# Attention with an off-by-one softmax and a cosine router on one core: one transposition for the rests of q and k, a shorter router product, and GpSimd's adds tied to VectorE

## The chip, the cores and the metric

The kernel runs on one core of a Trainium2 chip, as one launch. The metric is the device time in microseconds (us) of that launch; lower is better. A profile is one execution recorded by the hardware profiler. In it PE is TensorE (PEld its weight loads), DVE is VectorE, ACT is ScalarE, POOL is GpSimd, and SP is SyncE, which here only issues transfers. A Q behind an engine's name (POOLq) is that engine's instruction queue.

## What is computed

First attention over 8 batches, 12 heads, 448 positions and head size 64, whose softmax has an extra term in its denominator. Its result, laid out as 3584 tokens of 768 numbers, goes through a router that picks one of 8 experts for each token by cosine similarity, and through that expert's two layers.

```python
def _attn_ref(q, k, v):                      # (8, 12, 448, 64) each
    scores = scale * np.matmul(q, k.transpose(0, 1, 3, 2))
    m = np.max(scores, axis=-1, keepdims=True)
    e = np.exp(scores - m)
    attn = e / (np.sum(e, axis=-1, keepdims=True) + np.exp(-m) + 1e-09)
    return np.matmul(attn, v)

def _moe_ref(x, expert_emb, tau, w1, w2):    # N, D, E, F = 3584, 768, 8, 1024
    xn = x / (np.linalg.norm(x, axis=-1, keepdims=True) + 1e-06)
    en = expert_emb / (np.linalg.norm(expert_emb, axis=-1, keepdims=True) + 1e-06)
    logits = xn @ en.T / tau
    expert_idx = np.argmax(logits, axis=1)
    # ... gate_w: the softmax probability of the chosen expert ...
    for e in range(E):
        h = np.maximum(x[mask] @ w1[e], 0.0)
        out[mask] = gate_w[mask, None] * (h @ w2[e])
```

## The kernel before

The kernel is one hand-made schedule. Work is cut into 48 head pairs g (six to a batch); a pair has eight slots of program order. `put(slot, fn)` files a piece of work under a place in that order, and the pieces are emitted by ascending slot. So slots fix the order in which each engine gets its instructions; they are not times. Every engine runs its own queue in order.

448 positions are three blocks of 128 and a rest of 64. Scores are made transposed: keys on partitions, queries along the row, and the two heads of a pair on the two halves of the array's rows. For a pair: q and k are transposed on TensorE into PSUM, `kt` is copied out by ScalarE and `qt` by VectorE; three score blocks j (both heads each) and one block for the rests of both heads go through the exponential on ScalarE and a subtraction of one on VectorE (`em`, `emx`); `attend` multiplies them with v; `recip` makes the reciprocal denominator in two ScalarE steps (`rd`); `normalise` makes x on VectorE.

```python
LAG = 2 * NP                                   # NP = 6 pairs a batch
FILL = ((2.8, 5.3, 5.4), (2.8, 5.4))
...
    nc.gpsimd.tensor_tensor(out=vs[:], in0=vs[:], in1=t.v[:, :, 2, :], op=ALU.add)
    nc.gpsimd.tensor_tensor(out=vs[:], in0=vs[:], in1=t.v[:, :, 3, :], op=ALU.add)
    k.va[n] = vs


def front_qk(k, g, s):
    nc = k.nc
    n, i = g // GP, g % GP
    t = k.ld[n]
    ps = k.big.tile([128, 2, 512], F32, name="big", tag="big")
    for m, x, r in ((0, t.qm, t.qr[:, 2 * i : 2 * i + 2, :]), (1, t.km, t.kr[:, i, :])):
        for j in range(3):
            nc.tensor.transpose(ps[:, m, 128 * j : 128 * j + 128], x[:, j, 2 * i : 2 * i + 2, :], k.ident[:])
        nc.tensor.transpose(ps[:, m, SM:512], r, k.ident[:])
    def k_out():
        kt = k.qt.tile([128, 512], F32R, name="kt", tag="kt")
        nc.scalar.copy(out=kt[:], in_=ps[:, 1, :])
        k.kts[g] = kt

    def q_out():
        qt = k.qt.tile([128, S], F32R, name="qt", tag="qt")
        nc.vector.tensor_copy(out=qt[:], in_=ps[:, 0, 0:S])
        k.qts[g] = qt
    k.put(s + 1.1, k_out)
```

The rest of k was loaded into a tile of zeros with the two heads on the diagonal (rows 0 to 63 in columns 0 to 63, rows 64 to 127 in columns 64 to 127), so its transposition puts zeros beside each head. The rest of q has its own tile, of which half the rows are zero.

```python

    k.put(pa, exp)


def attend(k, g, s):

    nc = k.nc
    va = k.vab[g % 2]
    ps = k.av.tile([128, 2, 512], F32, name="av", tag="av")
    for h in range(2):
        r = slice(64 * h, 64 * h + 64)
        nc.tensor.matmul(
            ps[:, h, 0:S], lhsT=va[r, 3, h : h + 2, :], rhs=k.ems[g, 3][r, :], start=True, stop=False,
        )
    for j in range(3):
        for h in range(2):
            nc.tensor.matmul(
                ps[:, h, 0:S], lhsT=va[:, j, h : h + 2, :], rhs=k.ems[g, j][:, h, :],
                start=False, stop=(j == 2),
            )

    i = g % GP
    nc.tensor.matmul(ps[:, 0, S : S + 1], lhsT=k.va[g // GP][:, 2 * i : 2 * i + 2, :], rhs=k.ones_f[:], start=True, stop=True)
    rd = k.rdp.tile([128, 2, S], F32, name="rd", tag="rd")
    k.avs[g] = ps, rd

    def recip():
        nc.scalar.activation(rd[:], ps[:, :, 0:S], ACT.Ln, bias=1.0, scale=1.0 / (S + 1.0))
        nc.scalar.activation(rd[:], rd[:], ACT.Exp, scale=-1.0)

    k.put(s + 2.3, recip)
```

The router needs, for each token, the products with the 8 expert embeddings and the sum of squares over all six x of a batch. Four products run side by side on 32 columns of the array each, q = 0 and 1 with the embeddings, q = 2 and 3 with ones and the squares:

```python


def square(k, g):
    x = k.xs[g]
    xs = k.xsp.tile([128, S], F32, name="xs", tag="xs")
    if g < LAG - 1:
        k.nc.gpsimd.tensor_tensor(out=xs[:], in0=x[:], in1=x[:], op=ALU.mult)
    else:
        k.nc.scalar.activation(xs[:], x[:], ACT.Square)
    k.xs[g] = (x, xs)


def router_mm(k, b, s):

    nc = k.nc
    ps = k.big.tile([128, 512], F32, name="rmm", tag="big")
    for r in range(3):
        for q in range(4):
            c = 3 * (q % 2) + r
            x = k.xs[b * NP + c][q // 2]
            nc.tensor.matmul(
                ps[32 * q : 32 * q + 32, 0:S], lhsT=(k.en[:, c, :] if q < 2 else k.ones32[:]), rhs=x[:],
                start=(r == 0), stop=(r == 2),
            )
    for c in range(NP):
        k.xs.pop(b * NP + c)
    k.put(s + 1.9, lambda: nc.scalar.copy(out=k.rr[:, 0:S], in_=ps[:, 0:S]))

```

The result is copied by ScalarE, transposed in four pieces (`router_tok`), and VectorE finds the best expert of each token. Tokens are counted by a matmul with ones, the expert with most tokens in the batch is read into a GpSimd register, and GpSimd then fetches that expert's weights in seven transfers. Its layers, the MoE of the batch, are 15 chunks of matmuls (8 of the first layer, 7 of the second), which fill TensorE between the steps of attention pairs from LAG pairs on. Until then, dummy matmuls on the identity (`warm`) stand in their place. Where tokens choose other experts, a loop at the end adds those; the counts decide that while the kernel runs.

```python
# in pipeline(k)
    for n in range(NG * B):                    # a load covers two pairs
        ...
        put(s + 1.2, lambda n=n: sum_v(k, n))  # three GpSimd adds over v
    for g in range(G):
        s = g * NSLOT
        put(s - NSLOT + 4.2, lambda g=g, s=s - NSLOT + 4.2: front_qk(k, g, s))
        put(s + 0.8, lambda g=g: front_v(k, g))
        for j, o, pa, pv in ((0, 0, 0.3, 1.5), (1, 0.05, 0.4, 2.6), (2, 5.2, 6, 7.7), (3, 0.15, 2.6, 7)):
            put(s + o, lambda g=g, j=j, pa=s + pa, pv=s + pv: scores(k, g, j, pa, pv))
        s += NSLOT
        put(s + 0.1, lambda g=g, s=s: attend(k, g, s + 0.1))
        put(s + 4.75, lambda g=g, s=s: normalise(k, g, s + 4.75))
        put(s + 7.1, lambda g=g: square(k, g))
    put(-NSLOT, lambda: warm(k, 24))
    ...
# PSUM pools: work 2 x 1 bank, big 2 x 2 banks, av 1 x 2 banks
```

The softmax here doesn't subtract the row's maximum and nothing guards it: scores larger than these inputs give would overflow.

## Time and profile before

| what | value |
|---|---|
| time, median of 3 | 430.42 us (430.19 to 431.25) |
| span of the profiled execution | 430.1 us |
| instructions | 7384 |
| mean transfer rate | 162 GB/s |

A line of a group gives the kernel's line, the engine and operation, the tile written and the tiles read, their shape and type and how often it ran; behind the bar the busy time in us and the mean of one in ns, and then the idle time of the engine just before them and who ended most of it. The mean of a matmul is its latency, not its distance from the next. A line of the chain in order of time gives start, length and what ran; the chain is followed back from the last instruction, at each step to what released it. VectorE's largest groups, for instance:

```profile
L241 DVE TENSOR_SCALAR em<-e 128x896 fp32r<-128x896 f32 x144 | 96.9, 687 | 7.2 <-ACT e L233 6.8
L286 DVE SCALAR_TENSOR_TENSOR x<-av,rd 64x448 f32<-64x448 f32 x96 | 66.3, 691 | 46.7 <-ACT rd L274 36.4
L200 DVE CAST qt<-big 128x448 fp32r<-128x448 f32 x48 | 29.9, 624 | 24.1 <-ACT kt L195 22.8
```

Here x waited 46.7 us in all, mostly for the reciprocal rd, and qt 24.1 us, mostly for the end of ScalarE's copy kt.

### The profile page before, as it was taken

Reading aid. Unit: us, or ns where it says so; the run is one execution under the profiler, and the core shown is the slowest. Engines: PE = TensorE matmul, PEld = TensorE weight load, DVE = VectorE, ACT = ScalarE, POOL = GpSimd, SP = SyncE. Lnnn points to the kernel's source line nnn. Section 1 sums busy time; section 2 is a strip of 40 time slices with the busy share of each in tenths; the row PEclk is TensorE's granted clock in tenths of the full one; section 3 lists DMA queues with packets and bytes.
Section 4 is the critical chain, followed back from the end, with each engine's and each line's share of the span. In section 5 each row is a group of like instructions: output and inputs, shape, how many; then the busy total and the mean of one; then the engine's idle time right before and its main releaser. Section 6 shows DMA issues by size and latency. Waiting matters only on the chain.

```text
span 430.1 us, 7384 instructions
## 1 busy us (share of the span) xinstructions
PE 400.0 (93%) x2430; PEld 248.1 (58%) x2430; DVE 314.8 (73%) x658; ACT 305.3 (71%) x440; POOL 171.7 (40%) x242
## 2 busy tenths in 40 slices
PE   8878987879999999999999999999999999998885
PEld 3555554646556656665666656665666566644443
DVE  1697878789689769887787868976988778754222
ACT  1777776777788977978788878897698878751111
POOL 4043315754359106740377024910675037504500
PEclk9998999899999999999999999999999999999999
DMA  8775552997489964998399938997499508853973
GB/s 168 175 179 123 131 128 65 179 181 158 99 173 216 257 164 96 232 198 232 81 232 199 254 96 152 218 240 198 79 230 203 170 2 135 160 131 52 231 141 130
DMA packets 133690, 69.76 MB, mean 162 GB/s; under 512 B 99849, under 2 KB 127497, under 8 KB 133649
## 3 DMA queue, kind: packets, MB, share of 16 engines
q1 hardware_dynamic: 115392, 43.63, 40.0%
q0 software_dynamic: 16384, 25.17, 34.6%
q10 hardware_dynamic: 1872, 0.46, 0.6%
q8 instruction: 20, 0.33, 0.3%
q14 instruction: 22, 0.17, 0.1%
HBM read 83.39 MB, written 16.52 MB: 232 GB/s over the span
## 4 chain that ended last, share of the span: by engine, by line
PE 56%; DVE 20%; ACT 11%; issue 5%; POOL 4%; DMA 3%; POOLq 1%; DVEq 0%; ACTq 0%
PE av L262 11%; PE work L513 10%; PE work L485 8%; PE big L222 7%; DVE x L286 5%; PE big L191 4%; PE rmm L317 4%; DVE em L241 4%; DVE qt L200 4%; ACT e L233 3%; ACT rd L274 3%; DMA w<-in_moe_w_dram 3%; ACT rd L273 3%; PE work L629 2%; PE work L532 2%
## 5 line engine op out<-in xcount | busy, mean ns | idle before, releaser
L233 ACT ACTIVATE e<-big 128x896 f32<-128x896 f32 x144 | 127.6, 921 | 32.1 <-PE big L222 31.4
L241 DVE TENSOR_SCALAR em<-e 128x896 fp32r<-128x896 f32 x144 | 96.9, 687 | 7.2 <-ACT e L233 6.8
L286 DVE SCALAR_TENSOR_TENSOR x<-av,rd 64x448 f32<-64x448 f32 x96 | 66.3, 691 | 46.7 <-ACT rd L274 36.4
L485 PE MATMUL work<-xb,w 128*128 128x448 bf16 x384 | 79.7, 353 | 1.3 <-DMA w<-in_moe_w_dram 0.8
L262 PE MATMUL av<-em,vab 128*128 128x448 f32 x288 | 73.1, 391 | 0.0
L513 PE MATMUL work<-w,h 128*128 128x384 bf16 x384 | 68.4, 326 | 4.8 <-DMA w<-in_moe_w_dram 2.0
L222 PE MATMUL big<-qt,kt 64*128 64x448 f32 x288 | 56.8, 435 | 15.8 <-DVE qt L200 15.0
L357 POOL TENSOR_TENSOR nrm<-nrm,half 128x4 f32<-128x4 f32 x8 | 8.5, 1068 | 134.0 <-DVE nrm L339 134.0
L262 PEld LDWEIGHTS av<-em,vab 128*128 128x128 f32 x288 | 51.5, 192 | 16.2 <-issue 13.1
L485 PEld LDWEIGHTS <-w 128*128 128x128 bf16 x384 | 34.9, 98 | 39.4 <-issue 9.8
L273 ACT ACTIVATE rd<-av 128x896 f32<-128x896 f32 x48 | 44.1, 919 | 17.4 <-PE av L268 11.2
L445 POOL DMA_DIRECT2D w<-in_moe_w_dram x56 | 45.2, 809 | 27.0 <-issue 23.0
L513 PEld LDWEIGHTS <-h 128*128 128x128 bf16 x384 | 35.5, 98 | 31.5 <-issue 9.3
L222 PEld LDWEIGHTS big<-qt,kt 64*128 64x128 f32 x288 | 24.3, 184 | 43.1 <-ACT e L233 14.4
L200 DVE CAST qt<-big 128x448 fp32r<-128x448 f32 x48 | 29.9, 624 | 24.1 <-ACT kt L195 22.8
L274 ACT ACTIVATE rd<-rd 128x896 f32<-128x896 f32 x48 | 45.7, 952 | 1.5
L195 ACT CAST kt<-big 128x512 fp32r<-128x512 f32 x48 | 28.1, 585 | 12.1 <-PE big L192 12.0
L503 DVE TENSOR_SCALAR y<-work,g 128x384 f32<-128x384 f32 x32 | 19.6, 614 | 15.4 <-PE work L513 11.2
L629 PE MATMUL work<-ident 128*128 128x512 bf16 x96 | 28.6, 426 | 2.0 <-POOL ident masks.py:199 1.7
L493 DVE TENSOR_SCALAR h<-work 128x448 bf16<-128x448 f32 x40 | 24.6, 617 | 6.8 <-PE work L485 6.7
L209 DVE CAST vab<-vld 128x512 fp32r<-128x512 f32 x48 | 29.4, 612 | 0.0
L303 POOL TENSOR_TENSOR xs<-x 128x448 f32<-128x448 f32 x11 | 10.3, 933 | 40.5 <-DVE x L286 34.7
(103 smaller groups left out, 569.2 us busy)
## 6 DMA issues: line engine op xcount, KB each, us to landing
w<-in_moe_w_dram POOLq DMA_DIRECT2D x24, 512.0 KB, 7.9
w<-in_moe_w_dram POOLq DMA_DIRECT2D x32, 384.0 KB, 7.8
qm<-in_q_dram SPq DMA_DIRECT2D x72, 128.0 KB
vld<-in_v_dram SPq DMA_DIRECT2D x24, 384.0 KB
out_dram<-y SPq DMA_DIRECT2D x48, 192.0 KB
km<-in_k_dram SPq DMA_DIRECT2D x69, 128.0 KB
qrest<-in_q_dram SPq DMA_DIRECT2D x24, 64.0 KB
vld<-in_v_dram SPq DMA_DIRECT2D x48, 32.0 KB
```

What stands on the lines that cost most here:

```text
L200: nc.vector.tensor_copy(out=qt[:], in_=ps[:, 0, 0:S])
L222: nc.tensor.matmul(ps[:, h, 0:S], lhsT=kt[64 * h : 64 * h + 64, 128 * j : 128 * j + 128], rhs=qt[64 * h : 64 * h + 64, :], start=True, sto ...
L233: nc.scalar.activation(e[:], ps[:, :, 0:S], ACT.Exp, scale=scale)
L241: nc.vector.tensor_scalar_sub(em[:], e[:], 1.0)
L262: nc.tensor.matmul(ps[:, h, 0:S], lhsT=va[:, j, h : h + 2, :], rhs=k.ems[g, j][:, h, :], start=False, stop=(j == 2),)
L273: nc.scalar.activation(rd[:], ps[:, :, 0:S], ACT.Ln, bias=1.0, scale=1.0 / (S + 1.0))
L274: nc.scalar.activation(rd[:], rd[:], ACT.Exp, scale=-1.0)
L286: nc.vector.scalar_tensor_tensor(out=x[r, :], in0=ps[r, h, 0:S], scalar=ps[r, 0, S : S + 1], in1=rd[o, h, :], op0=ALU.add, op1=ALU.mult,)
L445: k.nc.gpsimd.dma_start(w[:], src)
L485: nc.tensor.matmul(ps[:, 0:S], lhsT=w1[c // 2][:, c % 2, 128 * f : 128 * f + 128], rhs=xb[:, c, :], start=(c == 0), stop=(c == NP - 1),)
L513: nc.tensor.matmul(ps[:, 0:SM], lhsT=hs[f][:, 128 * t : 128 * t + 128], rhs=w2[f // 2][:, f % 2, SM * n : SM * n + SM], start=(f == 0), st ...
L629: nc.tensor.matmul(ps[:], lhsT=idb[:, 0:128], rhs=idb.unsqueeze(1).broadcast_to([128, 2, 256]), start=True, stop=True)
```

## The change

Five things are done together. The rests of q and k of a head are loaded one above the other (q on rows 0 to 63, k on rows 64 to 127) and go through one transposition; two small VectorE copies put k's part into `kt`, which now has two fixed buffers whose zeros are written once. The squares of pairs 1 to 4 of a batch are added up on VectorE onto the first one, so that the router product has two accumulation steps instead of three. GpSimd's adds and squares get a dependence on the last subtraction of one on VectorE, so that they run while VectorE reads PSUM. The product for the rest scores of the next pair stands between the two parts of `attend`. And the slots of several pieces move: `qt` now stands ahead of `normalise`, MoE starts one pair earlier (LAG 11) with another spread of its chunks, and the router's later steps come later. The diff, cut where only names or the same lines move:

```diff
 NG = 3
-LAG = 2 * NP
-FILL = ((2.8, 5.3, 5.4), (2.8, 5.4))
+LAG = 2 * NP - 1
+FILL = 2 * ((2.8, 5.3, 5.4),) + ((2.8,), (2.8, 5.4)) + 2 * ((2.8, 5.3, 5.4),)
 NSLOT = 8
...
 def build_consts(k):
...
-        kr = pool.tile([128, GP, 128], F32, name=f"krest{s}")
-        nc.vector.memset(kr[:], 0.0)
...
+        kt = pool.tile([128, 512], F32R, name=f"kt{s}")
+        for h in range(2):
+            nc.vector.tensor_scalar_mul(
+                kt[64 * h : 64 * h + 64, S - 64 * h : 512 - 64 * h], k.ones_f[64 * h : 64 * h + 64, 0:1].broadcast_to([64, 64]), 0.0
+            )
+        k.kt.append(kt)
...
             )
-    nc.sync.dma_start(t.qr[0:64, :, :], k.q[b, h0 : h0 + 2 * GP, SM:S, :].rearrange("h p d -> p h d"))
-    keng.dma_start(t.kr[0:64, :, 0:64], rest2(k.k, 0))
-    keng.dma_start(t.kr[64:128, :, 64:128], rest2(k.k, 1))
+    for eng, h, src in ((nc.sync, 0, k.q), (keng, 1, k.k)):
+        eng.dma_start(t.r[64 * h : 64 * h + 64, :, :], src[b, h0 : h0 + 2 * GP, SM:S, :].rearrange("h p d -> p h d"))
     k.ld[n] = t
...
-def sum_v(k, n):
+def sum_v(k, n, js):
     nc, t = k.nc, k.ld[n]
-    vs = k.vsp.tile([128, 2 * GP, DH], F32, name="vs", tag="vs")
-    nc.gpsimd.tensor_tensor(out=vs[:], in0=t.v[:, :, 0, :], in1=t.v[:, :, 1, :], op=ALU.add)
-    nc.gpsimd.tensor_tensor(out=vs[:], in0=vs[:], in1=t.v[:, :, 2, :], op=ALU.add)
-    nc.gpsimd.tensor_tensor(out=vs[:], in0=vs[:], in1=t.v[:, :, 3, :], op=ALU.add)
-    k.va[n] = vs
+    if js[0] == 1:
+        k.va[n] = k.vsp.tile([128, 2 * GP, DH], F32, name="vs", tag="vs")
+    vs = k.va[n]
+    for j in js:
+        k.behind(nc.gpsimd.tensor_tensor(out=vs[:], in0=(vs[:] if j > 1 else t.v[:, :, 0, :]), in1=t.v[:, :, j, :], op=ALU.add))
...
     t = k.ld[n]
-    ps = k.big.tile([128, 2, 512], F32, name="big", tag="big")
-    for m, x, r in ((0, t.qm, t.qr[:, 2 * i : 2 * i + 2, :]), (1, t.km, t.kr[:, i, :])):
+    pq = k.big.tile([128, 512], F32, name="tq", tag="big")
+    pk = k.work.tile([128, 512], F32, name="tk", tag="work")
+    for ps, x in ((pq, t.qm), (pk, t.km)):
         for j in range(3):
-            nc.tensor.transpose(ps[:, m, 128 * j : 128 * j + 128], x[:, j, 2 * i : 2 * i + 2, :], k.ident[:])
-        nc.tensor.transpose(ps[:, m, SM:512], r, k.ident[:])
+            nc.tensor.transpose(ps[:, 128 * j : 128 * j + 128], x[:, j, 2 * i : 2 * i + 2, :], k.ident[:])
+        if x is t.qm:
+            nc.tensor.transpose(pq[:, SM:512], t.r[:, 2 * i : 2 * i + 2, :], k.ident[:])
+    kt = k.kt[g % 2]
+    k.kts[g] = kt
+
     def k_out():
-        kt = k.qt.tile([128, 512], F32R, name="kt", tag="kt")
-        nc.scalar.copy(out=kt[:], in_=ps[:, 1, :])
-        k.kts[g] = kt
+        nc.scalar.copy(out=kt[:, 0:SM], in_=pk[:, 0:SM])
...
         qt = k.qt.tile([128, S], F32R, name="qt", tag="qt")
-        nc.vector.tensor_copy(out=qt[:], in_=ps[:, 0, 0:S])
+        nc.vector.tensor_copy(out=qt[:], in_=pq[:, 0:S])
         k.qts[g] = qt
+
+    def r_out():
+        for h in range(2):
+            r = slice(64 * h, 64 * h + 64)
+            nc.vector.tensor_copy(out=kt[r, SM + 64 * h : S + 64 * h], in_=pq[r, S:512])
+
     k.put(s + 1.1, k_out)
-    k.put(s + 2.1, q_out)
+    k.put(s + 0.5, q_out)
+    k.put(s + 0.5, r_out)
...
-            nc.vector.tensor_scalar_sub(em[:], e[:], 1.0)
+            k.last = nc.vector.tensor_scalar_sub(em[:], e[:], 1.0)        # emx likewise
...
         )
-    for j in range(3):
-        for h in range(2):
-            nc.tensor.matmul(
-                ps[:, h, 0:S], lhsT=va[:, j, h : h + 2, :], rhs=k.ems[g, j][:, h, :],
-                start=False, stop=(j == 2),
-            )
-
-    i = g % GP
-    nc.tensor.matmul(ps[:, 0, S : S + 1], lhsT=k.va[g // GP][:, 2 * i : 2 * i + 2, :], rhs=k.ones_f[:], start=True, stop=True)
     rd = k.rdp.tile([128, 2, S], F32, name="rd", tag="rd")
     k.avs[g] = ps, rd
+
+    def rest():
+        for j in range(3):
+            for h in range(2):
+                nc.tensor.matmul(
+                    ps[:, h, 0:S], lhsT=va[:, j, h : h + 2, :], rhs=k.ems[g, j][:, h, :],
+                    start=False, stop=(j == 2),
+                )
+        i = g % GP
+        nc.tensor.matmul(ps[:, 0, S : S + 1], lhsT=k.va[g // GP][:, 2 * i : 2 * i + 2, :], rhs=k.ones_f[:], start=True, stop=True)
...
+    k.put(s + 0.04, rest)
     k.put(s + 2.3, recip)
...
+def on_pool(g):
+    return g < LAG - 1 and g % NP < NP - 1
+
+
 def square(k, g):
+    b, c = g // NP, g % NP
     x = k.xs[g]
-    xs = k.xsp.tile([128, S], F32, name="xs", tag="xs")
-    if g < LAG - 1:
-        k.nc.gpsimd.tensor_tensor(out=xs[:], in0=x[:], in1=x[:], op=ALU.mult)
+    tag = "xs" if c else "acc"
+    xs = k.xsp.tile([128, S], F32, name=tag, tag=tag, bufs=(3 if c else 1))
+    if on_pool(g):
+        k.behind(k.nc.gpsimd.tensor_tensor(out=xs[:], in0=x[:], in1=x[:], op=ALU.mult))
     else:
...
+def square_add(k, g):
+    acc = k.xs[g - g % NP][1]
+    k.nc.vector.tensor_tensor(out=acc[:], in0=acc[:], in1=k.xs[g][1][:], op=ALU.add)
+
+
 def router_mm(k, b, s):
...
     ps = k.big.tile([128, 512], F32, name="rmm", tag="big")
-    for r in range(3):
+    for r in range(2):
         for q in range(4):
-            c = 3 * (q % 2) + r
-            x = k.xs[b * NP + c][q // 2]
+            x = k.xs[b * NP + 3 * r + q][0] if q < 3 else k.xs[b * NP + (NP - 1) * r][1]
             nc.tensor.matmul(
-                ps[32 * q : 32 * q + 32, 0:S], lhsT=(k.en[:, c, :] if q < 2 else k.ones32[:]), rhs=x[:],
-                start=(r == 0), stop=(r == 2),
+                ps[32 * q : 32 * q + 32, 0:S], lhsT=(k.en[:, 3 * r + q, :] if q < 3 else k.ones32[:]), rhs=x[:],
+                start=(r == 0), stop=(r == 1),
             )
...
     nc, p = k.nc, k.rp
-    tp = k.big.tile([128, 4, 128], F32, name="tok", tag="big")
+    tp = k.work.tile([128, 4, 128], F32, name="tok", tag="work")
     for t in range(4):
...
     # router_logits: squares in one column of four, logits in three, where it was two and two
-    nc.vector.reduce_sum(out=nrm[:], in_=tp[:, :, 64:128:32], axis=AX.X)
+    nc.vector.tensor_copy(out=nrm[:], in_=tp[:, :, 96])
...
     k.put = put
+    k.last = None
+
+    def behind(ins):
+        if k.last is not None:
+            k.tc.add_manual_dep(
+                ins.ins, k.last.ins.name, mybir.DependencyInfo(mybir.DependencyClass.Sync, mybir.DependencyReason.DATA),
+                reason="port",
+            )
+
+    k.behind = behind
     put(4.6, lambda: build_late_consts(k))
...
         put(max(-NSLOT, s - 5 * NSLOT + 1.1), lambda n=n: load_v(k, n))
-        put(s + 1.2, lambda n=n: sum_v(k, n))
+        if n:
+            put(s - NSLOT + 4.69, lambda n=n: sum_v(k, n, (1, 2)))
+            put(s + 4.69, lambda n=n: sum_v(k, n, (3,)))
+        else:
+            put(1.2, lambda: sum_v(k, 0, (1, 2, 3)))
     for g in range(G):
...
         put(s + 0.8, lambda g=g: front_v(k, g))
-        for j, o, pa, pv in ((0, 0, 0.3, 1.5), (1, 0.05, 0.4, 2.6), (2, 5.2, 6, 7.7), (3, 0.15, 2.6, 7)):
+        rest = (3, 0.12, 2.3, 2.7) 
+        for j, o, pa, pv in ((0, 0, 0.3, 1.5), (1, 0.05, 0.4, 2.6), (2, 5.2, 6, 7.7), rest):
             put(s + o, lambda g=g, j=j, pa=s + pa, pv=s + pv: scores(k, g, j, pa, pv))
...
         put(s + 4.75, lambda g=g, s=s: normalise(k, g, s + 4.75))
-        put(s + 7.1, lambda g=g: square(k, g))
-    put(-NSLOT, lambda: warm(k, 24))
+        put(s + NSLOT + (4.68 if on_pool(g) else 2.35), lambda g=g: square(k, g))
+        if 0 < g % NP < NP - 1:
+            put(s + 2 * NSLOT + 0.6, lambda g=g: square_add(k, g))
+    put(-NSLOT, lambda: warm(k, 18))
     for g in range(LAG):
...
         s = ((b + 1) * NP + 1) * NSLOT
-        put(s + 2.75, lambda b=b, s=s: router_mm(k, b, s + 2.75))
+        put(s + 2.85, lambda b=b, s=s: router_mm(k, b, s + 2.75))
         put(s + 7.9, lambda b=b, s=s: router_tok(k, b, s + 7.9))
...
         put(s + 0.9, lambda b=b: router_pow(k, b))
-        put(s + 3.5, lambda b=b: router_count(k, b))
-        put(s + 4.3, lambda b=b: router_index(k, b))
-        for i, o in enumerate((4.4, 10, 16, 25, 31, 37, 43)):
+        put(s + 6.9, lambda b=b: router_count(k, b))
+        put(s + 7.05, lambda b=b: router_index(k, b))
+        for i, o in enumerate((7.1, 10.5, 14, 20, 26, 32, 38)):
             put(s + o, lambda b=b, i=i: fetch(k, b, i))
-        put(s + 4.5, lambda b=b: router_exp(k, b))
-        put(s + 7.2, lambda b=b: router_act(k, b))
+        put(s + 7.2, lambda b=b: router_exp(k, b))
+        put(s + 10.38, lambda b=b: router_act(k, b))
         s += NSLOT
-        put(s + 3.5, lambda b=b: keep_rows(k, b))
-        put(s + 5.5, lambda b=b: keep_xb(k, b))
+        put(s + 6.95, lambda b=b: keep_rows(k, b))
+        put(s + 7.0, lambda b=b: keep_xb(k, b))
         put(s + 6, lambda b=b, s=s: router_gate(k, b, s + 6))
...
     for b in range(B):
-        pos = [((b * NP + LAG + i) * NSLOT, o) for i in range(NP) for o in FILL[i % 2]]
+        pos = [((b * NP + LAG + i) * NSLOT, o) for i in range(NP) for o in FILL[i]]
         for (s, o), fn in zip(pos, moe_chunks(k, b), strict=True):
...
-    n.xsp = pool("xsp", 6)
+    n.xsp = pool("xsp", 3)
...
-    n.yp = pool("yp", 5)
+    n.yp = pool("yp", 7)
```

## The prediction

> **What bounds the kernel now.** I read the page first (busy shares, then the chain that ended last), then busy time by stage, then the chain in order of time inside one stage, and last the timeline around single waits.
>
> ```profile
> PE 400.0 (93%) x2430; PEld 248.1 (58%) x2430; DVE 314.8 (73%) x658; ACT 305.3 (71%) x440; POOL 171.7 (40%) x242
> ...
> PE 56%; DVE 20%; ACT 11%; issue 5%; POOL 4%; DMA 3%; POOLq 1%; DVEq 0%; ACTq 0%
> ```
>
> TensorE is busy 93% but carries only 56% of the chain. So some stages hang on another engine, and the stage view must say which (start to end in us, length, then busy us and instruction count of PE, PEld, DVE, ACT, POOL; granted clock, DMA share, GB/s):
>
> ```profile
> 30.00:60.00 30.00, 26.27 (x141) 17.40 (x142) 26.12 (x47) 23.70 (x32) 9.64 (x12) 0.94 0.56 134
> 60.00:107.00 47.00, 40.48 (x232) 25.36 (x231) 38.05 (x74) 33.73 (x47) 25.60 (x32) 0.96 0.72 142
> 201.00:248.00 47.00, 46.37 (x292) 29.46 (x291) 37.82 (x80) 38.59 (x57) 19.82 (x27) 1.00 0.89 194
> 386.00:393.00 7.00, 5.31 (x32) 2.78 (x29) 3.33 (x18) 1.62 (x3) 1.25 (x2) 1.00 0.00 0
> ```
>
> Three regimes. From about 100 to 340 us TensorE is full (46.37 of 47 us): a batch, six head pairs, takes 46.84 us (router products start at 201.24 and 248.08 in the chain). Before 107 us TensorE has holes and its clock falls to 0.94 to 0.96. After 384 us the last router decides when the last weights may be fetched: the DMA share is 0.00 from 386 to 393. The early holes are a loop, seen in the chain in order of time (start, us, what):
>
> ```profile
> 19.07 0.93 ACT rd L273
> 20.02 0.96 ACT rd L274
> 20.98 0.03 issue
> 21.00 0.68 DVE x L286
> 21.70 0.70 DVE x L286
> 22.40 0.03 issue
> 22.43 0.64 DVE qt L200
> 23.07 0.14 issue
> 23.20 0.68 PE big L222 x4
> ```
>
> Two reciprocal steps, the normalisation of pair g, and only then the copy qt of a later pair, which was transposed long before; the next scores wait for qt, and the next attention product stands behind those scores in TensorE's queue. The attention products (17.49 and 24.19 us) are 6.7 us apart through this loop. The groups that the change touches:
>
> ```profile
> L191 PE MATMUL big<-ident,qm 128*128 128x128 f32 x144 | 23.9, 275 | 0.0
> L192 PE MATMUL big<-ident,krest 128*128 128x128 f32 x48 | 13.1, 273 | 0.0
> L317 PE MATMUL rmm<-x,en 128*32 128x448 f32 x96 | 19.6, 543 | 0.0
> L317 PE MATMUL rmm<-xs,ones 128*32 128x448 f32 x96 | 19.6, 543 | 0.0
> ```
>
> Their means are latencies. What one takes from a full TensorE is the step from start to start: 0.11 us for a transposition, and 2.39 us for a whole router product (24 records of 12 products).
>
> **What the Trainium skill says.** First, "SBUF — State Buffer", section "SBUF: two separate sides": VectorE and GpSimd share a port pair, held exclusively for a whole instruction by whichever comes first, where VectorE runs a two-port mode or has two SBUF inputs. The trace agrees, on one and the same copy:
>
> ```profile
> 185.08 1.00 POOL L180 TENSOR_TENSOR vs<-vs,vld 128x256 f32<-128x256 f32 x1
> ...
> 185.39 0.97 DVE L209 CAST vab<-vld 128x512 fp32r<-128x512 f32 x1
> ...
> 192.46 0.42 DVE L209 CAST vab<-vld 128x512 fp32r<-128x512 f32 x1
> ```
>
> Second, "VectorE: DVE Perf Modes", section "Why PSUM operands drop a tier": an operand in PSUM rules the two-port mode out, since PSUM has one read port. The trace fits: qt takes 0.62 us for 448 elements out of PSUM, em the same 0.62 us for 896 out of SBUF. So a GpSimd add beside qt or x costs VectorE nothing. Third, "TensorE: Matmul & The Clock Gate", Part 3, section "The mechanism": a weight load overlaps running products only where it goes to other row groups. The trace agrees: the first full load of the attention product behind the two half-height products waits 0.30 us.
>
> **The change part by part.**
>
> Transpositions: 7 instead of 8 a pair, 48 x 0.11 = 5.3 us of TensorE. ScalarE copies 384 columns instead of 512; by the slope between its copy of 512 columns (0.585 us) and its exponential of 448 (0.527) that is about 0.1 us a pair. VectorE gains two 64x64 copies a pair, about 0.15 to 0.2 us each (48 columns took 0.208): 12 x 0.17 = 2.0 us a batch.
>
> Router product: 8 products for 12, in two accumulation steps for three: 2.39 x 2/3 = 1.6 us, so 0.8 us a batch, 6.4 in all. VectorE gains four adds of 448 elements with two SBUF inputs, about 0.55 us each (qt's rate): 2.2 us a batch.
>
> Rest scores inside the product: the rest scores' product (0.187 us of columns) now hides the next weight load, and no longer stands behind the one-column product, where its own 0.19 us load lay open; a 0.10 us bf16 load stands there instead. About 0.1 us a pair, 5 us in all.
>
> GpSimd's adds: the excess over the undisturbed time is 144 x (0.687 - 0.62) = 9.6 us for em, 48 x (0.612 - 0.42) = 9.2 for vab, 48 x (0.507 - 0.38) = 6.1 for emx, 48 x (0.463 - 0.38) = 4.0 for xb: 29 us, 3.6 a batch. Most of it should go, which pays for the 4.2 us a batch that VectorE gains. VectorE stays near 38 us a batch.
>
> Order, which the title does not name: qt now stands ahead of x on VectorE. And in the program qt no longer waits for ScalarE's copy of k, as it did while both were one PSUM tile (the chain has kt 10.79 + 0.59, then qt at 11.40), but for TensorE alone. That cuts the loop shown above. What is left runs over the single attention buffer: reciprocals 1.9, filler, transpositions, qt and rest copies (these run beside the reciprocals), x 1.4, half-height and rest products 0.55, attention product 1.42 + 0.12, and some 0.4 of hand-overs: 5.7 to 6.0 us a pair for 6.7. In the full stage the waits for qt (5.6 + 0.8 us in the four batches from 154 to 342) go as well, 1.6 us a batch at most.
>
> MoE one pair earlier (LAG 11): as much TensorE work, moved from the end into pair 11. The router group now has one filling chunk and the last router has no chunk ahead of its transposition. Warm-up: 18 matmuls for 24. In the trace the first dozen run at 0.43 us and the last at 0.22, so six fewer let the first transposition start about 1.3 us earlier, if q and k have landed.
>
> The sum by stages:
> - Start: -1.3 us.
> - Pairs 0 to 6: 41.5 us now, 6.0 x 6 + 0.5 = 36.5: -5.
> - Pairs 6 to 12: 46.5 us now, with one router and a first MoE group: about 40: -6.5.
> - Pairs 12 to 42, five batches of 46.84: TensorE loses 0.66 + 0.8 + 0.6 = 2.06 us each, giving 44.8. The router group needs chunk 1.24 + router 1.6 + transpositions 0.55 + qt and rests 1.0 + x 1.4 + attention 2.1 = 7.9 us through VectorE, half a microsecond over its TensorE work. Some qt waits go. I take 45.0: -9.2.
> - Last pairs: -1.5.
> - End: the router's chain is 0.8 shorter and two chunks (2.4 us, of which about 1.3 lay on the chain) no longer stand ahead of its transposition; the third weight fetch is issued before the rows are kept. The first fetch came 12.6 us after the last attention product, by the same rows it should come after 10.7; the fetches took 24.5 us to land, perhaps 23: -3.5.
>
> Together -27, or 403. Each new dependency can bring a stall that I have not seen, so I keep 23 of the 27: 407 us.
>
> **The rivals.**
> - VectorE or ScalarE becomes the bound. For: 4.2 us a batch of new VectorE work; a VectorE queue that now stops for the transpositions before x; ScalarE at 38.6 of 47 us. Against: neither would pass 39 of 45 us. If the contention stays, VectorE is at 42 and the full stage gains 1 us a batch: about 415.
> - GpSimd waits behind VectorE and delays the weights. For: MoE starts one pair earlier while the counting is placed 3.4 eighths of a pair later, so fetch-to-use shrinks to about 2.5 pairs, 18 us, and the DMA share of 0.89 rises to 0.93. Against: a fetch lands in 7.9 us and GpSimd is busy 42%. If it bites, some 1 to 2 us a batch: about 417.
> - The transposed k in the two-buffer work pool blocks a chunk: the third chunk of a pair needs the buffer that ScalarE's copy of k frees, 3.05 us behind the attention product; TensorE has 3.75 us of other work before it. It should not wait; if it does, half a microsecond a pair: about 425.
> - Early stages stay as they are because ScalarE (5.6 us a pair) or input transfers hold them: then 11 us of the gain are lost, 416.
>
> **Range and chances.** The reduction of TensorE's work alone (5.3 + 6.4 + 5 = 17 us, three quarters of it in the full stage) gives about 415 with the early loop unbroken. All terms give 403, less with the qt waits gone entirely. Range 397 to 419. Faster by over 2% means under 421.8; it takes two rivals at once to miss it: 0.90. Within 2%: 0.08. Slower: 0.02.
>
> **What would show it.** The distance of router products in the full stage: near 45.0 us right, 46 or more wrong. Attention products of pairs 1 to 6 about 6.0 us apart, with L200 gone from the chain's early part. Mean of em near 0.63 us and vab near 0.43 (contention gone). The router product at 1.6 us. First transposition near 8.4 us. TensorE's busy time near 383. Wrong: idle time of TensorE ahead of the third chunk released by the k copy, idle of ScalarE ahead of the router's exponential over 2 us, or MoE products waiting for weights before 380 us.

## The result and the profile after

| | before | changed |
|---|---|---|
| time, median | 430.31 us (429.37 to 431.25) | 443.69 us (442.97 to 446.05) |
| ratio, 95% interval | | 1.032 (1.027 to 1.037) |
| a batch of the full stage, mean of five | 46.8 us | 50.3 us |

The change makes the kernel 3.2% slower; 407 us had been predicted. Busy shares and the chain that ended last, of the changed kernel:

```profile
PE 394.7 (89%) x2306; PEld 244.2 (55%) x2306; DVE 326.8 (74%) x787; ACT 296.7 (67%) x442; POOL 161.8 (36%) x237
...
PE 47%; ACT 19%; DVE 17%; issue 6%; DMA 5%; POOL 5%; SPq 0%; POOLq 0%; ACTq 0%; DVEq 0%
```

TensorE has 124 matmuls and 5 us less to do, but its share of the chain fell from 56 to 47% and ScalarE's rose from 11 to 19%. Busy time by stage (start to end, length, then busy us and count of PE, PEld, DVE, ACT and POOL; granted clock, DMA share, GB/s):

```profile
30.00:60.00 30.00, 28.09 (x166) 17.26 (x166) 26.20 (x61) 25.40 (x35) 10.21 (x13) 1.00 0.56 135
60.00:107.00 47.00, 41.79 (x232) 25.82 (x230) 38.95 (x93) 35.71 (x51) 23.55 (x31) 0.96 0.79 156
201.00:248.00 47.00, 42.43 (x258) 27.14 (x250) 37.29 (x90) 33.38 (x52) 18.14 (x26) 0.96 0.81 168
```

The early stage is better: 166 matmuls in the 30 us where there were 141, at full clock. The full stage is worse: TensorE, busy 46.37 of 47 us before, is busy 42.43, for 258 matmuls where there were 292, at clock 0.96. Stage by stage, between the same landmarks of the two profiled executions (spans of 430.1 and 444.5 us):

| stage | before | changed | predicted change | measured |
|---|---|---|---|---|
| up to the first attention product | 17.49 | 17.25 | -1.3 | -0.2 |
| from there to that of pair 6 | 41.5 | 36.4 | -5 | -5.1 |
| first to second router product | 46.5 | 46.0 | -6.5 | -0.5 |
| second to seventh (five batches) | 234.4 | 251.7 | -9.2 | +17.3 |
| seventh to eighth | 42.1 | 45.4 | -1.5 | +3.3 |
| from the eighth to the end | 46.2 | 45.8 | -3.5 | -0.4 |

Of the 41 us between the sum of 403 and the result, 26.5 lie in the full stage. Two things are seen there. The first is in the chain in order of time for an ordinary pair (start, length, what):

```profile
237.21 2.43 PE work L504 x12
239.64 0.60 PE big L229 x4
240.24 0.20 PE av L264 x2
240.44 0.42 PE work L235
240.85 0.04 issue
240.89 0.91 ACT e L240
241.81 0.43 ACT e L242
242.24 0.46 ACT xs L320
242.70 0.82 ACT rd L281
243.52 0.02 issue
243.54 0.61 ACT rd L282
244.15 0.25 issue
244.40 0.54 ACT h L514
244.93 0.04 issue
244.97 2.43 PE work L504 x12
```

This is a ring, closed after 7.76 us: two MoE chunks, score products, then five pieces of ScalarE (an exponential, the one for the rests L242, the square L320, both reciprocal steps) and the eviction h of a MoE chunk, which lets the next two chunks go. Why those wait is in the timeline of the same stretch, TensorE and ScalarE (start, length, engine, line, form; in brackets idle time and releaser):

```profile
242.03 1.30 PE L504 MATMUL work<-xb,w 128*128 128x448 bf16 x6
...
243.60 0.49 PE L189 MATMUL tk<-ident,km 128*128 128x128 f32 x3
...
244.40 0.53 ACT L514 ACTIVATE h<-work 128x448 bf16<-128x448 f32 x1
...
244.97 2.43 PE L504 MATMUL work<-xb,w 128*128 128x448 bf16 x12 [0.49 <-ACT h L514]
```

The pool `work` has two buffers, taken in turn. Before, a pair with three chunks took them as rest scores, chunk 1, chunk 2, chunk 3, so chunk 2 needed the buffer of the rest scores. Now the transposed k (tk) stands in the row: rest scores, chunk 1, tk, chunk 2, chunk 3. So chunk 2 needs the buffer of chunk 1, whose products are over at 243.3 us but whose eviction stands behind the square and the reciprocals and starts at 244.40.

The second is the pair after the router's. The timeline:

```profile
216.39 0.24 POOL L384 TENSOR_TENSOR l<-l,nrm 128x32 f32<-128x32 f32 x1
216.66 0.23 ACT L390 ACTIVATE l<-l 128x32 f32<-128x32 f32 x1 [2.34 <-POOL l L384]
216.80 0.90 ACT L281 ACTIVATE rd<-av 128x896 f32<-128x896 f32 x1
219.20 2.29 PE L551 MATMUL work<-w,h 128*64 128x384 bf16 x16 [2.79 <-ACT y L524]
221.43 2.30 PE L532 MATMUL work<-w,h 128*128 128x384 bf16 x8
...
226.12 1.46 PE L532 MATMUL work<-w,h 128*128 128x384 bf16 x8
```

The router's exponential L390 now stands just ahead of the reciprocals (its slot is 10.38, the reciprocals' 2.4 of the next pair), and its operand comes from GpSimd, behind the counting, which the change placed later. ScalarE stands idle 2.34 us, the reciprocals and the eviction behind them (L524, of the second layer) come as much later, and TensorE has a hole of 2.79 us. Behind it the same 8 products take 2.30 us instead of 1.46, because the clock has fallen:

```profile
219.00:224.00 5.00, 4.80 (x28) 2.60 (x29) 2.98 (x9) 1.34 (x3) 3.96 (x6) 0.66 1.13 263
```

This is the view by stretches again; 0.66 is the clock granted in the 5 us behind the hole. The clock does not fall behind every such hole. From the two batches ahead of it in the same execution:

```profile
119.95 2.04 PE L551 MATMUL work<-w,h 128*64 128x384 bf16 x16 [2.32 <-ACT y L524]
...
170.12 1.49 PE L551 MATMUL work<-w,h 128*64 128x384 bf16 x16 [2.26 <-ACT y L524]
```

The holes are almost equally long. Behind the first the 16 products take 2.04 us and the next 8 take 2.56; behind the second 1.49 and 1.47, the times at full clock. The two batches took 50.2 and 48.5 us, so the fall of the clock costs some 1.7 us of a batch. Over the whole run the list of waits (who waits for whom, us in total, times, longest) has:

```profile
ACT l L390 <- POOL l L384: 20.1, 8, 3.3
PE work L551 <- ACT y L524: 16.6, 6, 3.7
```

ScalarE waited 20.1 us in eight batches, and TensorE 16.6 us in six holes. Before, ScalarE had the same wait (15.5 us in all), but behind the reciprocals, and the list of waits of the full stage shows no wait of TensorE that came of it.

The groups that the tied adds were meant for did what was expected of them:

```profile
L248 DVE TENSOR_SCALAR em<-e 128x896 fp32r<-128x896 f32 x144 | 86.9, 629 | 2.0 <-ACT e L240 1.5
L216 DVE CAST vab<-vld 128x512 fp32r<-128x512 f32 x48 | 21.6, 450 | 0.0
```

em fell from 687 to 629 ns and vab from 612 to 450.

### The profile page after: what moved, and what is told of

It is laid out like the page before. It is cut to its first block, busy times and chain, and to the rows that moved or that the text cites. A ratio compares the mean times of both kernels' runs of the same rounds, so it can differ in the third digit from the quotient of the medians.

```text
span 444.5 us, 7234 instructions
## 1 busy us (share of the span) xinstructions
PE 394.7 (89%) x2306; PEld 244.2 (55%) x2306; DVE 326.8 (74%) x787; ACT 296.7 (67%) x442; POOL 161.8 (36%) x237
## 4 chain that ended last, share of the span: by engine, by line
PE 47%; ACT 19%; DVE 17%; issue 6%; DMA 5%; POOL 5%; SPq 0%; POOLq 0%; ACTq 0%; DVEq 0%
PE work L504 12%; PE work L532 9%; DVE x L295 5%; PE av L273 5%; ACT rd L281 5%; ACT e L240 5%; PE big L229 4%; PE work L235 3%; DVE em L248 3%; PE rmm L336 3%; PE work L551 3%; DMA w<-in_moe_w_dram 2%; DVE qt L200 2%; POOL nrm L383 2%; ACT rd L282 2%
## 5 line engine op out<-in xcount | busy, mean ns | idle before, releaser
L248 DVE TENSOR_SCALAR em<-e 128x896 fp32r<-128x896 f32 x144 | 86.9, 629 | 2.0 <-ACT e L240 1.5
L532 PE MATMUL work<-w,h 128*128 128x384 bf16 x384 | 73.4, 343 | 2.9 <-ACT y L524 2.1
L273 PE MATMUL av<-em,vab 128*128 128x448 f32 x288 | 67.7, 371 | 0.0
L200 DVE CAST qt<-tq 128x448 fp32r<-128x448 f32 x48 | 30.0, 624 | 43.4 <-PE tq L191 43.0
L464 POOL DMA_DIRECT2D w<-in_moe_w_dram x56 | 45.2, 808 | 31.6 <-DVE em L248 20.7
L178 POOL TENSOR_TENSOR vs<-vs,vld 128x256 f32<-128x256 f32 x48 | 35.3, 736 | 52.3 <-issue 25.9
L178 POOL TENSOR_TENSOR vs<-vld 128x256 f32<-128x256 f32 x24 | 17.5, 728 | 88.4 <-PE av L278 69.5
L282 ACT ACTIVATE rd<-rd 128x896 f32<-128x896 f32 x48 | 45.7, 952 | 1.5
L522 DVE TENSOR_SCALAR y<-work,g 128x384 f32<-128x384 f32 x40 | 24.6, 616 | 24.4 <-PE work L532 14.9
L514 ACT ACTIVATE h<-work 128x448 bf16<-128x448 f32 x32 | 17.1, 534 | 20.2 <-PE work L504 20.2
L551 PE MATMUL work<-w,h 128*64 128x384 bf16 x128 | 14.4, 373 | 16.6 <-ACT y L524 16.6
L196 ACT CAST kt<-tk 128x384 fp32r<-128x384 f32 x48 | 22.6, 472 | 9.3 <-PE tk L189 9.2
```

What stands on the lines that cost most here:

```text
L178: k.behind(nc.gpsimd.tensor_tensor(out=vs[:], in0=(vs[:] if j > 1 else t.v[:, :, 0, :]), in1=t.v[:, :, j, :], op=ALU.add))
L200: nc.vector.tensor_copy(out=qt[:], in_=pq[:, 0:S])
L248: k.last = nc.vector.tensor_scalar_sub(em[:], e[:], 1.0)
L273: nc.tensor.matmul(ps[:, h, 0:S], lhsT=va[:, j, h : h + 2, :], rhs=k.ems[g, j][:, h, :], start=False, stop=(j == 2),)
L464: k.nc.gpsimd.dma_start(w[:], src)
L532: nc.tensor.matmul(ps[:, 0:SM], lhsT=hs[f][:, 128 * t : 128 * t + 128], rhs=w2[f // 2][:, f % 2, SM * n : SM * n + SM], start=(f == 0), st ...
```

## The experiments

My theory was the buffer in `work`, made worse by the router's exponential; the rivals were that VectorE's new work or the dependence of GpSimd's adds (the port waits) cost the time. All ratios are to the kernel before, with 95% intervals. "A batch" is the distance of the router's transpositions in the full stage: 46.8 us before; changed 48.5 to 51.6, in the mean 50.3.

### One part alone: k's transposition in the work pool

To the kernel before, only this is done; the rests, the router product, the squares, the slots and the adds stay.

```diff
-    ps = k.big.tile([128, 2, 512], F32, name="big", tag="big")
+    pq = k.big.tile([128, 512], F32, name="tq", tag="big")
+    pk = k.work.tile([128, 512], F32, name="tk", tag="work")
...
```

> The kernel before with one part of the change alone: the transposed k in a buffer of the work pool, q alone in the big pool. Buffer theory: a chunk now waits for the eviction two work buffers earlier, ordinary pairs 0.3 to 0.6 us longer, time 436 to 450 us. Order theory: ScalarE's order is as before, and qt no longer waits for ScalarE's copy of k, so 425 to 431 us.

Measured: 446.11 us, ratio 1.033 (1.028 to 1.037); a batch 49.3. The timeline shows the wait:

```profile
218.37 0.95 ACT L275 ACTIVATE rd<-rd 128x896 f32<-128x896 f32 x1
...
219.23 0.53 ACT L236 ACTIVATE e<-work 128x448 f32<-128x448 f32 x1
...
219.81 0.55 PE L192 MATMUL tk<-ident,km 128*128 128x128 f32 x3 [0.84 <-ACT e L236]
```

This part of the change, alone, loses as much as the whole change does (by other waits, so the equal size is chance). Here tk itself waits, for the exponential of the rest scores, which in the old order stands behind both reciprocals. The change moved that exponential ahead of the reciprocals, so that tk is free, and the wait went to the next in the row, chunk 2.

### The changed kernel with k's transposition back in the big pool

```diff
-    pq = k.big.tile([128, 512], F32, name="tq", tag="big")
-    pk = k.work.tile([128, 512], F32, name="tk", tag="work")
+    pqk = k.big.tile([128, 2, 512], F32, name="tqk", tag="big")
+    pq, pk = pqk[:, 0, :], pqk[:, 1, :]
```

> The changed kernel with the transposed k back in the second bank of q's own two-bank buffer, so that it takes no buffer of the two-buffer work pool. Buffer theory: the second chunk of a pair stands behind ScalarE's eviction of the first (and so behind both reciprocals) only because the transposed k took a turn in the work pool; ordinary pairs go from 7.8-8.1 us to about 7.3, 2 to 3 us a batch, time 420 to 428 us. Order theory (the exponential of the rests and the squares stand ahead of the reciprocals on ScalarE): nothing changes, 440 us or more. GpSimd theory: the same, 440 or more.

Measured: 432.68 us, 1.002 (0.999 to 1.005). The full stage did what the buffer theory says: a batch of 46.4 us, although ScalarE waits for GpSimd almost as long as before (19.4 us in all). The ring is gone: in an ordinary pair the chain holds nothing but TensorE, from one two-chunk piece to the next 7.23 us:

```profile
236.35 2.38 PE work L504 x12
...
243.58 2.38 PE work L504 x12
```

The early part gave the gain back: the first router transposition comes at 66.6 us instead of 59.2. The copy of k now waits for VectorE's copy of the rest out of the same PSUM tile, a wait that is not in the changed kernel's list, where they are two tiles; and each pair's loop is longer:

```profile
ACT kt L196 <- DVE kt L206: 34.8, 40, 8.6
```

### The router's exponential behind the reciprocals

```diff
-        put(s + 10.38, lambda b=b: router_act(k, b))
+        put(s + 14.02, lambda b=b: router_act(k, b))
```

> The changed kernel with only the router's exponential moved on ScalarE from ahead of the reciprocals to behind the next pair's third score block. Router theory: ScalarE's 2.3 us of waiting for GpSimd go, and with them TensorE's hole and its two chunks at half clock, 3 to 4 us a batch, seven times: 415 to 423 us. If the hole is only handed to the buffer wait behind it, 1 us a batch: 434 to 438. If the stall is beside the path: 443.

Measured: 422.82 us, 0.980 (0.976 to 0.984); a batch 46.5. The wait of ScalarE is gone, and the same products run without hole and at full clock. In the chain of this kernel, the pair after the router's:

```profile
210.49 1.49 PE work L551 x16
211.98 1.41 PE work L532 x8
```

One number in the program is worth 21 us. What is left is the ring, whose links come in the same order in this chain; between the two-chunk pieces of an ordinary pair (226.86 and 234.63 us) it takes 7.77 us. It closes in three of a batch's six pairs, and the chain around the router runs through VectorE instead. So that six rounds of 7.76 us are 46.6, where a batch takes 46.5, is in part chance.

### Both

Both edits above.

> The changed kernel with both of these edits. If buffer wait and router wait are separate and both real, a batch falls from 50.4 us to about 44.5 and the time to 398 to 408 us. If one of them explains everything, no better than the better of the two single edits. If the order of ScalarE's queue is what costs, above 425.

Measured: 424.13 us, 0.983 (0.977 to 0.990); a batch 45.7. My expectation took the two gains as a sum. They are not one: either edit alone brings the batch from 50.3 to about 46.5, both bring 0.8 more. ScalarE's wait reaches TensorE through the buffer; with either link cut, the holes of 2.3 to 3.7 us in the full stage are gone, and at most 0.9 us of one is left. The early part is 4 to 5 us slower, as with the transposition in the big pool alone. So I left tk in `work` and shortened the ring.

### The square out of the ring

To the kernel with the later exponential, ScalarE's square of x moved from between exponential and reciprocals to the end of the pair.

```diff
-        put(s + NSLOT + (4.68 if on_pool(g) else 2.35), lambda g=g: square(k, g))
+        put(s + (NSLOT + 4.68 if on_pool(g) else 7.1), lambda g=g: square(k, g))
```

> The kernel of e2 (router's exponential later) with ScalarE's squares moved back to where they stood before the change, behind the third score block, instead of ahead of the reciprocals. In e2 a batch still takes 46.5 us. Loop theory: an ordinary pair is held by one ring, two chunks on TensorE, scores, two exponentials, rest exponential, square, two reciprocal steps, eviction of the first chunk, and back; the square is 0.58 us of the 7.76, so a pair loses about 0.5 us, a batch goes to about 44.7 us and the time to 410 to 415. If TensorE or transfers bound e2, nothing moves: 421 to 424.

Measured: 414.96 us, 0.965 (0.959 to 0.971); a batch 45.2, against 45.0 predicted for the change. Taking 0.46 us from a ring of 7.76 gives 7.30. Where the ring still closes in this chain, from 223.80 to 231.18 us, it takes 7.38, little more than TensorE's own 7.23 for such a pair, and TensorE is nearly full again. The same stage of this kernel:

```profile
201.00:248.00 47.00, 45.83 (x287) 29.72 (x287) 41.48 (x100) 39.46 (x60) 19.87 (x28) 1.00 0.89 190
```

That is 287 matmuls where the changed kernel has 258, at clock 1.00. All of VectorE's new work is still in this kernel, so that work is not what made the changed kernel slower.

### Chunk 1 evicted by VectorE

To the kernel with the later exponential: chunk 1 is evicted by VectorE and chunk 2 by ScalarE, so that the buffer does not wait in ScalarE's queue.

```diff
-    late = {2.8: (4.7, False), 5.3: (7.3, True), 5.4: (8.5, True)}
+    late = {2.8: (4.69, True), 5.3: (7.3, False), 5.4: (8.5, True)}
```

> The kernel of e2 with the eviction of a pair's first chunk moved from ScalarE (behind the reciprocals) to VectorE, ahead of the copy of q, and that of the second chunk moved from VectorE to ScalarE. Buffer theory: the first work buffer comes free 1.2 us behind the attention product instead of 2.7, the wait of the second chunk goes, a batch at 44.3 to 45.3 us, 408 to 416 us. If the order of ScalarE's queue (rests and squares ahead of the reciprocals) is the bound and not the buffer, 419 to 424.

Measured: 418.44 us, 0.972 (0.967 to 0.977); a batch 45.4. The batch says that the buffer was the link; the time lies between the two expectations. With the square moved as well:

> Both edits of e5 and e6 on the kernel of e2. If each opens the same ring, no better than the better one; if the square holds the reciprocals and the eviction the buffer in rings of their own, some 3 us better. 405 to 414 us. TensorE's own work, 44.05 us a batch, is the floor.

Measured: 420.37 us, 0.975 (0.970 to 0.980), a batch 45.9: a miss, slower than either edit alone. In its ordinary pairs the chain holds nothing but TensorE (from 222.11 to 229.36 and 236.58 us, 7.24 us a pair), as it does with the eviction moved alone. The loss is thus elsewhere; the chain around its router runs through VectorE (`y`, `xb`, `vab`, em), which has 42.35 of 47 us to do, and GpSimd. Which of those waits decides was not tried.

### Without the port waits

To the changed kernel: the dependence of GpSimd's adds and squares on the last subtraction is left out. Nothing else changes.

> The changed kernel with one part undone: GpSimd's adds and squares keep their places in the order but no longer wait for VectorE's last subtraction. Port theory: the mean of em goes back from 0.63 towards 0.69 us and vab from 0.43 to about 0.6, and since VectorE is not the bound the time stays within 1% of 443. GpSimd theory (these waits delay the router's chain): GpSimd reaches the exponential's input earlier, 430 to 438 us.

Measured: 459.66 us, 1.068 (1.060 to 1.075). So the port waits are not the cause; without them the change would have lost more than twice as much. VectorE's groups in this kernel:

```profile
L248 DVE TENSOR_SCALAR em<-e 128x896 fp32r<-128x896 f32 x144 | 92.2, 666 | 1.1 <-ACT e L240 0.6
L216 DVE CAST vab<-vld 128x512 fp32r<-128x512 f32 x48 | 29.1, 607 | 0.0
```

With the waits they take 629 and 450 ns. The full-stage batch stays at about 50.9 us; the time goes early, where VectorE is on the loop: the first router transposition comes at 66.9 us instead of 59.2, the second at 116.3 instead of 104.5. The timeline there shows single collisions:

```profile
21.75 1.37 POOL L318 TENSOR_TENSOR acc<-x 128x448 f32<-128x448 f32 x1 [4.71 <-DVE x L295]
22.25 1.12 DVE L303 TENSOR_SCALAR xb<-x 128x448 bf16<-128x448 f32 x1
23.08 0.88 POOL L178 TENSOR_TENSOR vs<-vs,vld 128x256 f32<-128x256 f32 x1
23.29 0.96 DVE L216 CAST vab<-vld 128x512 fp32r<-128x512 f32 x1
```

xb lies beside a square of GpSimd, vab beside an add; their means in the changed kernel are 0.39 and 0.45 us. My expectation was that the waits hardly matter; that was wrong by 16 us.

### Toward a better version

Four more, from the kernel with the later exponential and the early square (414.96 us). First, only the squares of the first batch are left to GpSimd, and ScalarE does the others:

```diff
-    return g < LAG - 1 and g % NP < NP - 1
+    return g < NP - 1
```

> The kernel of e5 with the squares of pairs 6 to 9 on ScalarE instead of GpSimd (those of pairs 0 to 4 stay). In e5 the first two router products are still 46.1 us apart, and TensorE waits 3.2 us for an em that stands on VectorE behind a sum waiting for GpSimd, then runs at half clock. GpSimd-queue theory: GpSimd's squares and adds stand ahead of the mask that this sum reads; without four squares of 0.93 us it comes earlier, the distance falls to 42 to 44 us, time 411 to 413. If the wait is for the weight fetch's register load and issue instead, nothing moves: 414 to 416.

Measured: 414.36 us, 0.961 (0.955 to 0.968). The stretch between the first two router transpositions got 0.9 us shorter (46.06 to 45.17), the total did not move by more than its spread: inconclusive. Second, the old LAG of 12, with the pair of one chunk as the second of six (the squares stay where they were):

```diff
-LAG = 2 * NP - 1
-FILL = 2 * ((2.8, 5.3, 5.4),) + ((2.8,), (2.8, 5.4)) + 2 * ((2.8, 5.3, 5.4),)
+LAG = 2 * NP
+FILL = ((2.8, 5.3, 5.4), (2.8,), (2.8, 5.3, 5.4), (2.8, 5.4)) + 2 * ((2.8, 5.3, 5.4),)
```

> The kernel of e5 with MoE one pair later again (LAG 12, the single chunk kept in the router's pair, squares on GpSimd for the same pairs). Run-dry theory: with LAG 11 TensorE has used up the last but one batch's chunks before the last weights land, waits, and its clock falls to 0.72 for the first layer of the last batch; one pair of chunks more at the end fills that: the end from the last router transposition falls from 42.8 us to about 41 and everything ahead of it is unchanged or 1 us shorter, 411 to 413 us. If the end is bound by the router and the transfers alone, the end keeps its length: 414 to 416.

Measured: 414.47 us, 0.961 (0.957 to 0.965). The end after the last router transposition fell from 42.8 to 40.7 us, as expected. But it is 40.2 us in the kernel with ScalarE's squares too, which has the LAG of 11, so this fall cannot be put down to the LAG. A batch took some 0.5 us more, and the total stayed. Third, both together:

> Both edits of e9 and e10. They touch different stages, so their gains should add: 408 to 411 us if both theories hold.

Measured: 412.88 us (412.50 to 413.57), 0.957 (0.953 to 0.961): the lowest median of all, faster than both kernels, 1.9 us above the expected range. The medians of these four lie within 1.6 us. Fourth, to the one with ScalarE's squares: 28 dummy matmuls in the end, behind the chunks of the seventh MoE, while TensorE waits for the last weights.

```diff
+    put((7 * NP + LAG + 0) * NSLOT + 2.79, lambda: warm(k, 28))
```

> The kernel of e9 (LAG 11) with 28 dummy products on the identity (6 us) put behind the last but one batch's chunks, where TensorE waits for the last weights. Clock theory: the last batch's first layer runs at full clock, 44 products in 8.5 us instead of 10.9, so the time is 2 us below that of e9. If the dummies delay the first layer instead, 1 us above it; if transfers of the second layer's weights bound the end anyway, the same as e9.

Measured: 413.09 us, 0.959 (0.955 to 0.964). The first layer of the last batch in the early-square kernel (chain), in the one with ScalarE's squares, which has no dummies there (timeline), and in this one (chain):

```profile
389.04 10.92 PE work L504 x44
```

```profile
388.96 8.50 PE L504 MATMUL work<-xb,w 128*128 128x448 bf16 x44 [2.52 <-DMA w<-in_moe_w_dram]
```

```profile
381.75 6.04 PE work L648 x28
387.79 9.08 PE work L504 x48
```

48 products take 9.08 us behind the dummies, where 44 took 10.92 behind idle time in the early-square kernel (clock 0.72 from 390 to 397 us). But in the kernel to which the dummies were added, 44 took 8.50 us without them, at full clock, though TensorE had been idle for 2.52 us. From the last router transposition to the end that execution took 40.2 us, the one with dummies 41.3. So the lower clock explains the early-square kernel's long first layer; that the dummies mend it is not shown, and their gain, 1.3 us by the medians, is within the spread.

## Why the prediction was wrong

**The step that failed** is the third rival: the transposed k in the two-buffer pool "should not wait; if it does, half a microsecond a pair". I had asked whether the third chunk waits for the copy of k. It does not. But a tile added to a rotation of two shifts every later user by one, and I did not walk on to the second chunk, whose buffer changed from the rest scores' to the first chunk's. Nor did I walk ScalarE's queue from there: exponential, rests, square, two reciprocals, eviction, in that order. The ring so made is 7.76 us, where TensorE's own work in such a pair is 7.23; the steady loss by it alone (later exponential, square still inside) is 1.5 us a batch against the 45.0 predicted. With the transposed k out of that pool again, a batch fell from 50.3 to 46.4 us.

**A second wait was named but not counted.** "Idle of ScalarE ahead of the router's exponential over 2 us" stood among the signs and had no term in the sum. It measured 2.34 us in the batch shown, and cost more: 2.79 us of hole, then 24 products at a reduced clock (2.29 + 2.30 for 1.49 + 1.46, 1.6 us more). With the 46.5 us of the ring this makes 50.9; the batch shown took 50.7. The two together account for the full stage: with both loosened, by the later exponential and the early square, a batch takes 45.2.

Point by point:
- Full stage, 45.0 us a batch: the TensorE terms in it were right, since 45.2 is reached where the two waits are loosened; the batch measured 50.3. TensorE's busy time, 383 predicted, was 394.7 us with the stretches at lower clock, and is 385.5 in the early-square kernel.
- Rest scores inside the product, 0.1 us a pair: right. `attend` and the rest scores take 1.93 us of TensorE (0.20 + 0.40 + 1.21 + 0.12) for 2.05 (0.20 + 1.42 + 0.12 + 0.31). The reason given was too narrow: the loads of the attention product take 190 ns each, and yet its six products, all on 128 rows, take 1.21 us, 0.20 each. So here loads lie under products on the same rows too.
- Pairs 0 to 6, -5: right, -5.1. Attention products are 5.8 us apart (17.25, 23.06, 28.89), predicted 5.7 to 6.0, and the wait of scores for qt, which had closed the loop before, is gone from one of the two rounds that the chain shows between 17 and 29 us.
- Router product 1.6 us: 1.64. Contention: em 0.63 us and vab 0.45, as predicted; its worth of "3.6 a batch" of VectorE's time was little gain in the full stage, but without it the changed kernel takes 16 us more, most of it ahead of the second router. Here the trace bears out what the Trainium skill says of the shared port pair ("SBUF — State Buffer", section "SBUF: two separate sides"), that one of the two engines holds it while the other waits: em 629 ns for 666, vab 450 for 607.
- VectorE's new work was a little larger: 217 ns for a 64x64 copy (0.17 assumed), 634 for an add of squares (0.55). VectorE is not the bound in the changed kernel, busy 37 of 47 us. Nor did weights come late: no MoE product waits for them before 400 us.
- Start, -1.3: only -0.2. The first transposition started at 7.04 us (9.71 before, 8.4 predicted), but "if q and k have landed" did not hold: the one transposition of the rests waits for k's part as well as q's.

```profile
9.19 0.33 PE L191 MATMUL tq<-ident,qkrest 128*128 128x128 f32 x1 [1.66 <-DMA qkrest<-in_k_dram]
```

The first exponential of scores still came at 10.93 us instead of 12.60. Then the clock fell (0.89 in the mean of the first 15 us, 1.00 before), which I had not counted, and most of the gain was lost. Whether that hole or the six dummy matmuls fewer brought the fall was not tried; in the early-square kernel the hole was 1.44 us, the clock stayed at 1.00, and the first attention product came 0.6 us earlier.
- Pairs 6 to 12, -6.5: -0.5 was measured. TensorE has a hole of 2.97 us ahead of scores, for ScalarE's copy kt, and its clock falls to 0.89 from 72 to 88 us. The copy stands behind the reciprocals, and they behind ScalarE's wait of 3.32 us for the router's operand: it is the second wait above. Loosening the waits did not mend this stage (46.1 us in the early-square kernel): there VectorE waits 2.4 us for GpSimd, whose queue holds squares, v adds and weight fetches ahead of what the gate needs, and TensorE 3.2 us behind it. The term was mis-sized: it had no room for a GpSimd that does squares and the first router's work at once. In the three kernels with fewer squares on GpSimd that hole is 2.3 us, so the squares are a part of it.
- End, -3.5: -0.4. The 44 products of the last first layer, which wait for weights, started 19.0 us behind the start of the router's transposition (17.4 before). MoE one pair earlier took work from the place where it had bridged that landing; TensorE stood idle for 2.25 and 2.94 us (0.75 before), and the 44 products took 10.7 us at clock 0.79 (8.5 us at full clock before). With the older LAG those holes are gone. But in the kernel with ScalarE's squares the layer ran at full clock without the older LAG or dummies, so what decides the clock there stays open.
- Range: I took the terms as independent and left 4 us for stalls not seen. Two stalls in a row on one queue cost 5 us in every batch. Nor did it take "two rivals at once" to miss 421.8 us: the third alone stood at 425, outside the range.

## What to carry to other kernels

When a tile moves into a pool that rotates, write down the whole row of users for two rounds, name for each the one whose buffer it takes, and then follow the in-order queue of the engine that frees it; the added tile need not be the one that waits (alone it was tk, in the changed kernel chunk 2). A wait for a slow foreign engine belongs behind the pieces that close a loop, not ahead of them: one slot number was worth 21 us here. And where two waits lie in series through one buffer, removing either gives nearly the whole gain, so their gains must not be added.

## What the hardware showed unexpectedly

- TensorE's clock can fall behind a hole of 2 to 3 us, and need not: behind 2.79 us 16 products took 2.29 us for 1.49 and 8 of another form 2.30 for 1.46, behind 2.32 us it fell as well, but behind 2.26 us in the changed kernel and 2.52 us in the one with ScalarE's squares it stayed at 1.00. The length of the hole alone does not decide it. The Trainium skill ("TensorE: Matmul & The Clock Gate", section "HAM oscillation — how this bites in real kernels") warns of idle gaps beyond some 3.4 us; in these traces shorter ones do it, and the hole shown cost about one and a half times its length (2.79 + 1.6 us).
- VectorE operations that meet GpSimd's adds and squares can take two to three times their time (xb 1.12 us for 0.39, vab 0.96 for 0.45), and making GpSimd's adds and squares wait for VectorE's last subtraction was worth 16 us of 460.
- Left open: which wait in the router pair makes chunk eviction on VectorE and the early square slower together than alone, and why the time of the changed kernel with both transpositions in one tile varies so much (429 to 436 us).
